# Fused attention, gated convolution and mixing MLP on one core: new ranks, new delays, and a head's first score moved by one place

## The chip, the cores and the metric

One NeuronCore of a Trainium2 chip. The metric is device microseconds of one execution of the whole program; a kernel's time is the median of its runs. Engines are named as in the profile: PE (TensorE matmuls), PEld (its weight loads), DVE (VectorE), ACT (ScalarE), POOL (GpSimd), SP (the queue that issues DMAs).

## What is computed

Three blocks follow each other, with B = 4 batches, 8 heads, sequence 576, head size 64, model size 512. Cut to what matters:

```python
scores = where(causal, -1e9, q @ k.T / 8 + minimum(-(cum_i - cum_j), 0))   # cum = cumsum(max(s, 0))
x = softmax(scores) @ v                      # 4 x 576 x 512, heads side by side
gate = sigmoid(causal_conv5(x, conv_w))      # 5 taps per channel
x = (gate * (x @ w_val)) @ w_out
u = x + (x.transpose(0, 2, 1) @ U @ V).transpose(0, 2, 1)    # rank 32 mixing over the sequence
out = u + maximum(u @ w_ch1, 0) @ w_ch2      # 512 -> 2048 -> 512
```

## The kernel before

Everything lives transposed in one tile `uT` (128 channels x 4 x 2304 tokens). Dense matmuls are made exact enough by splitting each operand into a rounded high part and the rest (`xh`/`xl`, `gvh`/`gvl`, `nh`/`nl`, `hh`/`hl`, weights `..h`/`..l`) and adding three products. Weights arrive as 64-bit words and are widened to two float parts by POOL and DVE in small steps (`widen`, lines 368 to 389); the DVE steps on integers there are called shifts in this document.

The 32 heads are taken one after the other, two of them a pair. For head n, `score` makes five row blocks S0 to S4 of scores, each followed by a row maximum on DVE (written into `P`, with `nm`) and an exp on ACT. One head later `trans` transposes the five blocks (T0 to T4) on PE into `pt`, and ACT or DVE copies them into `PTA` and `PTB`. After an odd head `attn_v` multiplies the pair by V in two parts A0 (reads `PTA`) and A1 (reads `PTB`), into the single accumulator `av`. Then DVE scales it into `X` by the row sums (`rs`, `wrs`), five taps of the convolution are accumulated in `av` again (`tap`, line 609), and a tanh on ACT writes the gate from `av` into `uT` (line 621). So the next pair's A0 can't start before this tanh. In timeline rows the tanh is `uT<-av`, a tap is `av<-X,cw,av`.

When a batch's eight heads are through, its dense work is laid between the next batch's heads: `values` (x times w_val, `d<-xh,wvh`; gating makes `gvh` on ACT and `gvl` on DVE), `outputs` (`d<-gvh,woh`), and the mixing, in which `uT` is transposed, split into `nh` (ACT) and `nl` (DVE), multiplied by U, split into `ast` by ACT and then DVE, and multiplied by V (`d<-V4h,ast`). For batch 0 the dense products start at head 10, for batch 1 at head 18, for batch 2 at head 26; the mixing falls into heads 14 to 16, 22 to 24 and 30 to 31. The last batch's dense work stands alone, with some MLP units laid between (`beside`, line 943), and from about 376 us only the MLP is left.

The order of the work is set three times over. The program emits steps on a clock of its own: ORDER and ORDER0 (lines 89, 90, used at line 785) give the order of scores, transpositions and products of a head, ORDER where the head being transposed is odd; `defer` (line 156) puts a step off by a delay from DT; SIDE, DENSE, R0 to R3 say how much side work goes between. Then a scheduler orders each engine's queue, and a kind's rank decides there: every operation goes through `Via` (line 118), which takes engine and rank from PLAN, or from FIRST for heads 0 to 8, and issues it with that priority (line 132). Last, each engine runs its queue in order. PSUM is short: six buffers `d` are shared by scores, transpositions and dense groups.

Lines: all operations with a rank other than 0 have line 132 (`Via`); with rank 0 they have the line of the call: 139 to 143 (`rnd`), 148 (`rest`), 375 (a POOL step of `widen`), 614 (a tap). In the changed kernel every line is 35 higher.

Of the kernel before, what the change touches and what calls it, by code (L numbers as in the profile page):

```python
# [19 lines left out]
DRAM = bass.MemoryType.DRAM  # L20


PLAN = {
    "pace": ("gpsimd", 0),
    "qk_hi": ("gpsimd", 2000),
    "qk_lo": ("gpsimd", 2000),
    "put": ("sync", 3000),
    "wd_rest": ("gpsimd", 100),
    "xh": ("gpsimd", 0),
    "xl": ("gpsimd", 500),  # L30
    "gh": ("scalar", 6000),
    "gl": ("vector", 0),
    "uh": ("gpsimd", -2000),
    "ul": ("gpsimd", -6000),
    "u4": ("vector", 0),
    "wd_a": ("gpsimd", 0),
    "wd_lim": ("gpsimd", 0),
    "wd": ("vector", -2000),
    "wd_hi": ("gpsimd", -2000),
    "wd_lo": ("gpsimd", 2000),  # L40
    "s": ("tensor", -6000),
    "max": ("vector", -2000),
    "exp": ("scalar", 6000),
    "t": ("tensor", 500),
    "pt00": ("scalar", 0),
    "pt10": ("scalar", 6000),
    "pt20": ("scalar", -500),
    "pt30": ("scalar", -6000),
    "pt40": ("scalar", -6000),
    "pt41": ("vector", 6000),  # L50
    "av": ("tensor", 6000),
    "rs": ("vector", -500),
    "wrs": ("gpsimd", 2000),
    "t_rb": ("tensor", 500),
    "rb": ("scalar", 6000),
    "x": ("vector", 2000),
    "tap0": ("scalar", 100),
    "tap": ("vector", 0),
    "tanh": ("scalar", -100),
    "d": ("tensor", 2000),  # L60
    "gv": ("vector", -100),
    "ox": ("scalar", 0),
    "tm": ("tensor", 6000),
    "nh": ("scalar", 0),
    "nl": ("vector", 100),
    "ah": ("scalar", -100),
    "al": ("vector", 0),
    "um": ("vector", 0),
    "c1": ("tensor", 100),
    "c2": ("tensor", -2000),  # L70
    "hh": ("scalar", 0),
    "hl": ("vector", 6000),
    "acc": ("vector", 6000),
}
R0 = 0.0
R1 = 0.0
R2 = 0.4
R3 = 6.0
DENSE = 36.0
DWAIT = 3.0  # L80
GROUPS = [2, 2, 3, 4, 3, 2]
RING = 7
PACED = False
SIDE = [7, 7, 3, 7]
WHOLE = [0, 1, 2, 3, 4, 5, 6, 7, 16, 30]
PB = [1, 1, 1, 2, 2]
XB = 1
FIRST = {"pt41": ["scalar", 500], "nl": ["vector", 500], "xh": ["gpsimd", 2000], "c2": ["tensor", 100], "max": ["vector", 2000], "rs": ["vector", 500], "t": ["tensor", 100], "rb": ["vector", 500], "av": ["tensor", 6000], "wd_rest": ["gpsimd", 2000]}
ORDER0 = "T0 S0 T1 T4 S1 T3 T2 S2 S3 S4"
ORDER = "T0 T1 S0 T2 T3 S1 S2 S3 T4 S4 A0 A1"  # L90
NPD = 6
DT = {"exp": 0.51, "xh": 0.96, "xl": 0.25, "tap": 1.5, "taps": 0.9, "tanh": 1.83, "gv": 4.3, "nl": 3.6, "rows": 10.0, "prep": 1.51}
WARM = 13


# [1 line left out]
def fused_kernel(ctx, tc, qT, kT, vP, s, wval, wout, convw, U, V, w1, w2, rows01, out):  # L97
# [20 lines left out]
    class Via:  # L118


        def __init__(self, kind):
            self.name, self.ahead = FIRST.get(kind, PLAN[kind]) if PLAN[kind][0] != "sync" and phase[0] <= 8 else PLAN[kind]
            self.engine = getattr(nc, self.name)
# [11 lines left out]
    def rnd(kind, o, i, by=1.0):  # L135

        eng = Via(kind)
        if eng.name == "scalar":
            eng.mul(o, i, by)  # L139
        elif eng.name == "vector" and by == 1.0:  # L140
            eng.tensor_copy(o, i)
        else:
            eng.tensor_scalar(o, i, by, 0.0, op0=ALU.mult, op1=ALU.add)
# [12 lines left out]
    def defer(dt, f, key=None):  # L156
        order[0] += 1
        later.append((clock["now"] + dt, order[0], f, key))
# [17 lines left out]
    def side_step(n=1):  # L176
        while n and side_work:
            more = side_work.popleft()()
            if isinstance(more, list):
                side_work.extendleft(reversed(more))  # L180
            else:
                n -= 1
# [7 lines left out]
    def advance(cost):  # L190
        clock["now"] += cost
        while later:
            x = min(later, key=lambda y: y[:2])
            if x[0] > clock["now"]:
                break
            later.remove(x)
            x[2]()
# [286 lines left out]
    def score(n, c):  # L484
# [26 lines left out]
        def exp():  # L511
# [4 lines left out]
            ready.add(("P", n, c))  # L516
        defer(DT["exp"] + W / 960.0, exp, "sc")

# [71 lines left out]
    def norm(pr):  # L590
# [8 lines left out]
        def split_hi():  # L599
            xh[b, p] = db.tile([P, S], F32R, tag=f"xh{p}", name=f"xh{p}", bufs=2 if p < XB else 1)  # L600
            xl[b, p] = db.tile([P, S], F32R, tag=f"xl{p}", name=f"xl{p}", bufs=2 if p < XB else 1)
            rnd("xh", xh[b, p], X[:, 4:])
            defer(DT["xl"], split_lo)

# [4 lines left out]
        def tap(k):  # L609

            if k == 0:
                Via("tap0").mul(g, X[:, 0:S], cw[:, p, 0:1])
            else:
                Via("tap").scalar_tensor_tensor(  # L614
                    g, X[:, k:k + S], cw[:, p, k:k + 1], g, op0=ALU.mult, op1=ALU.add,
                )
            defer(DT["taps"], lambda: tap(k + 1) if k < 4 else gate())

        def gate():

            Via("tanh").activation(G(b, p), g, AF.Tanh, scale=0.5)
            ready.add(("G", b, p))
        defer(DT["xh"], split_hi)
        defer(DT["tap"], lambda: tap(0))

# [19 lines left out]
    def values(b):  # L645
        halves = [slice(0, HS), slice(HS, S)]
        need(*[("wide", c) for c in range(NP)])
        until(*[("x", b, p) for p in range(NP)])
        for hf, cols in enumerate(halves):
            for m in range(NP):  # L650
                ps = psD.tile([P, 512], F32, tag="d", name="d")
                yield from products(
                    ps[:, 0:HS], wv, m, [xh[b, p][:, cols] for p in range(NP)], [xl[b, p][:, cols] for p in range(NP)],
                )
                until(("G", b, m))
                tmp = ps[:, 0:HS]
                Via("gv").scalar_tensor_tensor(tmp, G(b, m)[:, cols], 1.0, tmp, op0=ALU.add, op1=ALU.mult)
                gh = gvh[m, hf] = da.tile([P, HS], F32R, tag=f"gvh{m}{hf}", name="gvh")
                gl = gvl[m, hf] = da.tile([P, HS], F32R, tag=f"gvl{m}{hf}", name="gvl")

                def split(tmp=tmp, gh=gh, gl=gl, key=("gv", b, m, hf)):
                    rnd("gh", gh, tmp)
                    rest("gl", gl, tmp, gh)
                    ready.add(key)
                defer(DT["gv"], split)
        yield 0.0
# [95 lines left out]
    for n in range(NH + 1):  # L762
# [21 lines left out]
        ahead, before = n < NH, n > 0  # L784
        for x in (ORDER if m % 2 else ORDER0).split():
            kind, i = x[0], int(x[1])
# [20 lines left out]
        for cost, f, a in items:  # L807
# [3 lines left out]
            if n > 0:  # L811
                steps[0] += SIDE[(n > 8) + (n > 12) + (n > 17)] * cost / total
                side_step(int(steps[0]))
# [129 lines left out]
    def beside(gen, share):  # L943

        nonlocal owed
        for cost in gen:
            advance(cost)
            owed += R3 if cost == LULL else share
            while owed >= 1.0:
                next(first_blocks, None)  # L950
                owed -= 1.0

    while len(dense) > 1:
        beside(dense.pop(0)[1], 0.0)
    beside([0.0], R0)
    beside(values(B - 1), R1)
    advance(20.0)
    ctx_b.close()
    wb = ctx.enter_context(tc.tile_pool(name="wb", side="right", **reuse))
    beside(outputs(B - 1), R2)  # L960
    for k in (4, 5):
# [55 lines left out]
```

## Time and profile before

| | us |
|---|---|
| median of 3 runs | 757.72 |
| lowest, highest of the 3 | 756.76, 767.9 |
| the profiled execution | 759.31 |
| its span | 757.5 |
| TensorE busy in it | 732.2 |

The profiled execution is the one whose rows are read below. Its time includes 1.8 us around the span of the instructions. Times in rows are microseconds from the start of the span; in timeline rows the second number is the duration of the row's instructions and the square brackets tell how long the engine was idle before the row and what released it.

### The profile page before, as it was taken

To read this page: it belongs to the slowest core of one execution; us is meant where nothing else is said; L and a number is where in the kernel's file an instruction comes from. 1 tells how busy PE (TensorE), PEld (TensorE's weight loads), DVE (VectorE), ACT (ScalarE), POOL (GpSimd) and SP (SyncE) were. 2 spreads that over 40 slices of the span, in tenths; PEclk is the share of its full clock that TensorE was granted. 3 is DMA by queue.
4 is the path that set the end of the run, shared out by engine and by line. 5 is a ranking of instruction groups with operands and counts; after the bars stand their busy time and mean duration, and the time that the engine had idled before them with its cause. 6 is when DMAs were issued, how large, how long until landed. Compare 5 with 4: busy or idle time off the path is not lost.

```text
span 757.5 us, 12149 instructions
## 1 busy us (share of the span) xinstructions
PE 732.2 (97%) x4369; PEld 617.7 (82%) x4369; DVE 449.5 (59%) x1053; ACT 264.7 (35%) x718; POOL 340.8 (45%) x393
## 2 busy tenths in 40 slices
PE   8988999899999999999999999999999999999998
PEld 5666879678988998798788888888888888888887
DVE  6888887887668656651546776764462233323234
ACT  6776566756677567422110110110011011001110
POOL 2777677566544143550086877862660024100000
PEclk9999999999999999899999999999999999999999
DMA  4675354644556441010002222220120000000033
GB/s 121 188 200 160 90 136 111 174 118 128 143 130 154 107 98 35 29 57 1 0 1 84 84 84 82 86 83 29 34 79 28 1 29 0 1 1 1 0 112 139
DMA packets 27000, 59.39 MB, mean 78 GB/s; under 512 B 4648, under 2 KB 5288, under 8 KB 26940
## 3 DMA queue, kind: packets, MB, share of 16 engines
q1 hardware_dynamic: 26940, 58.61, 27.8%
q8 instruction: 35, 0.57, 0.3%
q14 instruction: 25, 0.20, 0.1%
HBM read 37.04 MB, written 5.31 MB: 56 GB/s over the span
## 4 chain that ended last, share of the span: by engine, by line
PE 85%; DVE 5%; DMA 3%; ACT 2%; POOL 2%; issue 1%; SPq 1%; POOLq 0%; DVEq 0%; ACTq 0%
PE d L132 42%; PE acc L132 26%; PE pt L132 7%; PE sc L132 5%; PE av L132 5%; DVE uT L132 2%; DVE P L132 1%; DMA qk<-in_kT 1%; DMA uT<-in_w 1%; DVE av L614 1%; DMA K<-Q 1%; ACT P L132 1%; SPq L132 0%; ACT PTA L132 0%; DMA K<-uT 0%
## 5 line engine op out<-in xcount | busy, mean ns | idle before, releaser
L132 PE MATMUL d<-u,w1h 128*128 128x512 f32 (+1 forms) x640 | 184.2, 371 | 0.0
L877 ACT ACTIVATE hh<-d 128x512 fp32r<-128x512 f32 (+1 forms) x80 | 44.1, 556 | 343.0 <-PE acc L132 177.3
L132 DVE SCALAR_TENSOR_TENSOR hl<-d,hh 128x512 fp32r<-128x512 f32 (+1 forms) x80 | 50.7, 635 | 152.9 <-ACT hh L877 152.8
L132 PEld LDWEIGHTS d<-u,w1h 128*128 128x128 f32 x640 | 116.1, 188 | 22.4
L132 PE MATMUL d<-u,w1l 128*128 128x512 f32 (+1 forms) x320 | 118.7, 371 | 0.0
L132 PE MATMUL acc<-hl,w2h 128*128 128x512 f32 (+1 forms) x320 | 104.5, 370 | 0.0
L132 PE MATMUL acc<-hh,w2h 128*128 128x512 f32 (+1 forms) x320 | 104.3, 371 | 0.2 <-DVE uT L132 0.2
L132 ACT ACTIVATE P<-P,nm 128x576 f32<-128x576 f32 (+4 forms) x160 | 89.1, 560 | 36.1 <-DVE nm L132 35.2
L132 PE MATMUL acc<-hh,w2l 128*128 128x512 f32 (+1 forms) x320 | 101.1, 369 | 0.0
L132 DVE TENSOR_TENSOR uT<-acc,uT 128x512 f32<-128x512 f32 (+1 forms) x120 | 70.1, 630 | 35.7 <-PE acc L132 30.4
L132 PE MATMUL sc<-K,Q 68*128 68x288 f32 (+13 forms) x384 | 87.3, 342 | 1.9 <-ACT PTA L139 1.8
L132 PE MATMUL pt<-ident,P 128*128 128x128 f32 x480 | 76.4, 284 | 5.2 <-ACT P L132 3.0
L132 DVE CUSTOM_DVE_ANT_0 P<-sc,causal 64x64 f32<-64x64 f32 (+4 forms) x160 | 64.9, 420 | 23.6 <-PE sc L132 21.4
L132 PEld LDWEIGHTS sc<-K,Q 68*128 68x128 f32 (+2 forms) x384 | 62.0, 193 | 9.3 <-ACT PTA L139 2.2
L132 PEld LDWEIGHTS d<-u,w1l 128*128 128x128 f32 x320 | 60.3, 188 | 11.2
L132 PEld LDWEIGHTS acc<-hh,w2h 128*128 128x128 f32 x320 | 58.8, 188 | 11.5 <-issue 0.6
L132 PEld LDWEIGHTS acc<-hl,w2h 128*128 128x128 f32 x320 | 59.0, 188 | 11.0 <-DVE hl L132 0.3
L132 PEld LDWEIGHTS acc<-hh,w2l 128*128 128x128 f32 x320 | 58.7, 188 | 10.5
L132 PEld LDWEIGHTS pt<-ident,P 128*128 128x128 f32 x480 | 54.8, 143 | 13.7 <-ACT P L132 5.4
L614 DVE SCALAR_TENSOR_TENSOR av<-X,cw,av 128x576 f32<-128x576 f32 x64 | 52.2, 815 | 3.0 <-ACT av L132 2.7
L132 DVE TENSOR_SCALAR scr<-scr 128x512 uint32<-128x512 uint32 x56 | 29.0, 519 | 29.9 <-POOL w1l L132 20.2
L132 ACT ACTIVATE PTB<-pt 128x384 f32<-128x384 f32 (+1 forms) x72 | 37.0, 522 | 10.3 <-PE pt L132 10.0
(125 smaller groups left out, 1285.5 us busy)
## 6 DMA issues: line engine op xcount, KB each, us to landing
raw<-in_w SPq DMA_DIRECT2D x28, 512.0 KB
K<-hi SPq DMA_DIRECT2D x44, 144.0 KB
Q<-hi SPq DMA_DIRECT2D x44, 144.0 KB
V<-in_vP SPq DMA_DIRECT2D x16, 320.0 KB
out<-uT SPq DMA_DIRECT2D x16, 256.0 KB
qk<-in_qT SPq DMA_DIRECT2D x22, 144.0 KB
qk<-in_kT SPq DMA_DIRECT2D x22, 144.0 KB
K<-Q SPq DMA_DIRECT2D x22, 144.0 KB
```

The source lines that it names most:

```text
L132: return f(*args, **kw)
L614: Via("tap").scalar_tensor_tensor(g, X[:, k:k + S], cw[:, p, k:k + 1], g, op0=ALU.mult, op1=ALU.add,)
L877: Via("hh").activation(h_, o, AF.Relu)
```

## The change

Only constants at the top of the file change; functions stay. The ranks in PLAN get other numbers (the engines stay), FIRST grows from 10 to 29 kinds, and these change:

```diff
-R0 = 0.0
+R0 = 0.13
-R2 = 0.4
-R3 = 6.0
+R2 = 0.38
+R3 = 9.68
-SIDE = [7, 7, 3, 7]
+SIDE = [7, 7, 2, 6]
-    "wd": ("vector", -2000),
+ 'wd': ['vector', 0],
-    "exp": ("scalar", 6000),
+ 'exp': ['scalar', -2000],
-ORDER = "T0 T1 S0 T2 T3 S1 S2 S3 T4 S4 A0 A1"
+ORDER = 'T0 S0 T1 T2 T3 S1 S2 S3 T4 S4 A0 A1'
-DT = {"exp": 0.51, "xh": 0.96, "xl": 0.25, "tap": 1.5, "taps": 0.9, "tanh": 1.83, "gv": 4.3, "nl": 3.6, "rows": 10.0, "prep": 1.51}
+DT = {'exp': 0.76,
+ 'xh': 0.72,
+ 'xl': 0.57,
+ 'tap': 1.65,
+ 'taps': 0.7,
+ 'tanh': 3.22,
+ 'gv': 4.08,
+ 'nl': 0.66,
+ 'rows': 8.9,
+ 'prep': 2.52}
```

So in ORDER the next head's S0 stands before T1 where it stood after it.

What that moves is told by the order of the engines' queues. On DVE, in the second head of the first mixing stage (head 15), this stood before; the TENSOR_SCALAR and SCALAR_TENSOR_TENSOR on `uT` are shifts of a weight slice, `P_92` is a score block with its maximum, `X_94` the scaled pair:

```order
L132 ISA P_92,nm<-sc,causal,nm 128x288
L132 ISA nm 128x1
L132 TENSOR_SCALAR uT<-uT 128x256
L132 SCALAR_TENSOR_TENSOR uT<-uT 128x256
L132 TENSOR_TENSOR nl<-pt,nh 128x512
L132 TENSOR_SCALAR uT<-uT 128x256
L132 SCALAR_TENSOR_TENSOR uT<-uT 128x256
L132 TENSOR_TENSOR X_94<-av,wrs 128x576
```

and this stands there now:

```order
L167 ISA P_92,nm<-sc,causal,nm 128x288
L167 ISA nm 128x1
L167 TENSOR_TENSOR nl<-pt,nh 128x512
L411 TENSOR_SCALAR uT<-uT 128x256
L167 TENSOR_TENSOR X_94<-av,wrs 128x576
L412 SCALAR_TENSOR_TENSOR uT<-uT 128x256
```

`nl` and `X` passed the shifts.

On ACT, in the same mixing stage (head 16), before; `P_91` and `P_87` are exps, `uT<-av` is the tanh:

```order
L132 ACTIVATE P_91,sums_97<-P_91,nm 128x448
L132 ACTIVATE PTA<-pt 128x3x128
L132 ACTIVATE ast<-d 128x512
L132 ACTIVATE PTB<-pt 128x4x128
L132 ACTIVATE uT<-av 128x576
L132 ACTIVATE P_87,sums_96<-P_87,nm 64x64
```

and now:

```order
L167 ACTIVATE PTA<-pt 128x3x128
L167 ACTIVATE ast<-d 128x512
L167 ACTIVATE uT<-av 128x576
L167 ACTIVATE P_87,sums_96<-P_87,nm 64x64
L167 ACTIVATE PTB<-pt 128x4x128
```

The tanh stands right behind `ast`, ahead of the `PTB` copy.

On ACT, where the dense products of batch 1 start (head 18), before:

```order
L132 ACTIVATE P_93,sums_96<-P_93,nm 128x576
L132 ACTIVATE uT<-av 128x576
L132 ACTIVATE gvh<-d 128x288 x2
L139 ACTIVATE PTA<-pt 128x64
L132 ACTIVATE PTA<-pt 128x2x128
L132 ACTIVATE gvh<-d 128x288 x2
L132 ACTIVATE PTA<-pt 128x3x128
L132 ACTIVATE P_87,sums_97<-P_87,nm 64x64
```

and now:

```order
L167 ACTIVATE P_93,sums_96<-P_93,nm 128x576
L174 ACTIVATE PTA<-pt 128x64
L167 ACTIVATE uT<-av 128x576
L167 ACTIVATE gvh<-d 128x288 x3
L167 ACTIVATE PTA<-pt 128x2x128
L167 ACTIVATE P_87,sums_97<-P_87,nm 64x64
L167 ACTIVATE PTA<-pt 128x3x128
```

The small `PTA` copy moved ahead of the tanh; three `gvh` and the exp now stand ahead of the last `PTA` copy, where four `gvh` and no exp stood.

## Rows read from the trace of the kernel before

**Rows 1.** The page: busy time of each engine over the span.
```profile
PE 732.2 (97%) x4369; PEld 617.7 (82%) x4369; DVE 449.5 (59%) x1053; ACT 264.7 (35%) x718; POOL 340.8 (45%) x393
```

**Rows 2.** Chain of waits, a dense stretch: start, us, engine and tile.
```profile
480.23 8.39 PE d L132 x36
```

**Rows 3.** Windows of the last stop before the values and of the MLP.
```profile
core 0: us, PE busy (x) PEld busy (x) DVE busy (x) ACT busy (x) POOL busy (x), PEclk, DMA share, GB/s
304.00:319.00 15.00, 13.52 (x80) 10.25 (x79) 9.64 (x25) 6.68 (x17) 7.60 (x7) 0.77 0.01 2
376.00:757.00 381.00, 378.23 (x1832) 316.34 (x1831) 184.99 (x305) 41.14 (x75) 149.38 (x152) 1.00 0.14 48
```

**Rows 4.** Waits of PE, 80 to 400 us: us in total, times, longest.
```profile
PE d L132 <- DVE ast L148: 2.4, 2, 1.5
PE av L132 <- ACT uT L132: 2.3, 2, 1.2
...
PE acc L132 <- DVE uT L132: 0.2, 1, 0.2
```

**Rows 5.** Timeline, 135 to 140 us, head 15.
```profile
135.22 0.60 ACT L139 ACTIVATE nh<-pt 128x512 fp32r<-128x512 f32 x1 [0.71 <-PE pt L132]
...
135.62 0.43 POOL L143 TENSOR_SCALAR uT<-uT 128x256 f32<-128x256 f32 x1 [3.01 <-DMA uT<-in_w]
...
136.49 1.40 POOL L132 TENSOR_TENSOR Q<-qk,hi 128x576 fp32r<-128x576 f32 x1
136.56 1.48 DVE L132 TENSOR_SCALAR uT<-uT 128x256 uint32<-128x256 uint32 x1 [1.31 <-POOL uT L375]
...
138.88 0.68 DVE L132 TENSOR_TENSOR nl<-pt,nh 128x512 fp32r<-128x512 f32 x1
...
139.49 0.28 DVE L132 TENSOR_SCALAR uT<-uT 128x256 uint32<-128x256 uint32 x1
139.62 0.51 PE L132 MATMUL d<-nl,U 128*128 128x512 f32 x1 [0.77 <-DVE nl L132]
```

**Rows 6.** Timeline, 146 to 150 us, head 16.
```profile
146.88 0.85 DVE L132 TENSOR_SCALAR uT<-uT 128x256 uint32<-128x256 uint32 x1
...
147.65 0.81 DVE L614 SCALAR_TENSOR_TENSOR av<-X,cw,av 128x576 f32<-128x576 f32 x1
147.72 0.59 ACT L132 ACTIVATE ast<-d 128x512 fp32r<-128x512 f32 x1
...
148.20 0.60 ACT L132 ACTIVATE PTB<-pt 128x512 f32<-128x512 f32 x1
...
148.68 0.67 ACT L132 ACTIVATE uT<-av 128x576 f32<-128x576 f32 x1
...
149.40 1.20 PE L132 MATMUL av<-PTA,V 128*64 128x320 f32 x12 [1.07 <-ACT uT L132]
```

**Rows 7.** Timeline, 156 to 160 us, head 17.
```profile
156.17 0.29 DVE L132 TENSOR_SCALAR uT<-uT 128x256 uint32<-128x256 uint32 x1 [0.72 <-POOL uT L375]
...
159.85 0.74 PE L132 MATMUL pt<-ident,P 128*128 128x128 f32 x5 [0.52 <-DVE nm L132]
```

**Rows 8.** Timeline, 108.6 us, the first score of head 12.
```profile
108.64 0.41 PE L132 MATMUL sc<-K,Q 68*128 68x64 f32 x2 [0.40 <-ACT PTA L139]
```

**Rows 9.** Timeline, 169 to 173 us, head 18.
```profile
169.39 0.65 ACT L132 ACTIVATE uT<-av 128x576 f32<-128x576 f32 x1 [1.27 <-DVE av L614]
...
170.24 0.77 ACT L132 ACTIVATE gvh<-d 128x288 fp32r<-128x288 f32 x2 [0.20 <-DVE d L132]
...
170.90 0.22 ACT L139 ACTIVATE PTA<-pt 128x64 f32<-128x64 f32 x1
...
171.17 0.41 PE L132 MATMUL sc<-K,Q 68*128 68x64 f32 x2 [1.36 <-ACT PTA L139]
...
172.48 0.34 ACT L132 ACTIVATE P<-P,nm 64x64 f32<-64x64 f32 x1
...
172.88 0.49 PE L132 MATMUL av<-PTA,V 128*64 128x320 f32 x2
```

More of the change, by code (lines that the diff above doesn't have):

```diff
@@ L20 @@
 DRAM = bass.MemoryType.DRAM
[L23 to L37, printed above, removed]
-    "wd": ("vector", -2000),
[L39 to L42, printed above, removed]
-    "exp": ("scalar", 6000),
[L44 to L74, printed above, removed]
@@ L75 @@
-R0 = 0.0
+PLAN = {'pace': ['gpsimd', -100],
+ 'qk_hi': ['gpsimd', 2000],
+ 'qk_lo': ['gpsimd', 100],
+ 'put': ['sync', 3000],
+ 'wd_rest': ['gpsimd', 0],
+ 'xh': ['gpsimd', 100],
+ 'xl': ['gpsimd', -2000],
+ 'gh': ['scalar', -2000],
+ 'gl': ['vector', 0],
+ 'uh': ['gpsimd', 2000],
+ 'ul': ['gpsimd', -500],
+ 'u4': ['vector', 0],
+ 'wd_a': ['gpsimd', 6000],
+ 'wd_lim': ['gpsimd', 0],
+ 'wd': ['vector', 0],
+ 'wd_hi': ['gpsimd', -6000],
+ 'wd_lo': ['gpsimd', 2000],
+ 's': ['tensor', -6000],
+ 'max': ['vector', -100],
+ 'exp': ['scalar', -2000],
+ 't': ['tensor', 500],
+ 'pt00': ['scalar', 0],
+ 'pt10': ['scalar', 6000],
+ 'pt20': ['scalar', 100],
+ 'pt30': ['scalar', 2000],
+ 'pt40': ['scalar', 2000],
+ 'pt41': ['vector', 6000],
+ 'av': ['tensor', 6000],
+ 'rs': ['vector', 2000],
+ 'wrs': ['gpsimd', -500],
+ 't_rb': ['tensor', 2000],
+ 'rb': ['scalar', -2000],
+ 'x': ['vector', -500],
+ 'tap0': ['scalar', 500],
+ 'tap': ['vector', 100],
+ 'tanh': ['scalar', -100],
+ 'd': ['tensor', -6000],
+ 'gv': ['vector', 2000],
+ 'ox': ['scalar', -2000],
+ 'tm': ['tensor', 500],
+ 'nh': ['scalar', 0],
+ 'nl': ['vector', 100],
+ 'ah': ['scalar', -6000],
+ 'al': ['vector', 500],
+ 'um': ['vector', 0],
+ 'c1': ['tensor', 100],
+ 'c2': ['tensor', -500],
+ 'hh': ['scalar', 0],
+ 'hl': ['vector', 6000],
+ 'acc': ['vector', -500]}
@@ L87 @@
 XB = 1
-FIRST = {"pt41": ["scalar", 500], "nl": ["vector", 500], "xh": ["gpsimd", 2000], "c2": ["tensor", 100], "max": ["vector", 2000], "rs": ["vector", 500], "t": ["tensor", 100], "rb": ["vector", 500], "av": ["tensor", 6000], "wd_rest": ["gpsimd", 2000]}
-ORDER0 = "T0 S0 T1 T4 S1 T3 T2 S2 S3 S4"
-ORDER = "T0 T1 S0 T2 T3 S1 S2 S3 T4 S4 A0 A1"
-NPD = 6
-DT = {"exp": 0.51, "xh": 0.96, "xl": 0.25, "tap": 1.5, "taps": 0.9, "tanh": 1.83, "gv": 4.3, "nl": 3.6, "rows": 10.0, "prep": 1.51}
+FIRST = {'pt41': ['scalar', 500],
+ 'nl': ['vector', 500],
+ 'xh': ['gpsimd', 0],
+ 'c2': ['tensor', -6000],
+ 'max': ['vector', 2000],
+ 'rs': ['vector', 500],
+ 't': ['tensor', 100],
+ 'rb': ['vector', 500],
+ 'av': ['tensor', 6000],
+ 'wd_rest': ['gpsimd', 2000],
+ 'ah': ['scalar', 0],
+ 'pt10': ['scalar', 0],
+ 'al': ['vector', 500],
+ 'xl': ['gpsimd', 500],
+ 'pt40': ['scalar', -2000],
+ 'gv': ['vector', 6000],
+ 'd': ['tensor', -2000],
+ 'pt00': ['scalar', 0],
+ 'gl': ['vector', 6000],
+ 'gh': ['scalar', 100],
+ 'hl': ['vector', 6000],
+ 'wd_hi': ['gpsimd', -6000],
+ 'u4': ['vector', -500],
+ 'pt20': ['scalar', -6000],
+ 'pace': ['gpsimd', -6000],
+ 'tm': ['tensor', -6000],
+ 'tap': ['vector', -2000],
+ 'qk_lo': ['gpsimd', -100],
+ 'wrs': ['gpsimd', 100]}
+ORDER0 = 'T0 S0 T1 T4 S1 T3 T2 S2 S3 S4'
+ORDER = 'T0 S0 T1 T2 T3 S1 S2 S3 T4 S4 A0 A1'
+NPD = 6
+DT = {'exp': 0.76,
[8 more added lines that the diff above has]
+ 'prep': 2.52}
 WARM = 13
```

## Prediction

> **What bounds the kernel now.** I read the page first. TensorE is busy for 732.2 of 757.5 us [rows 1], so only time in which it stands still, or runs at the lower clock, can be won or lost by a change of order. Busy time alone doesn't tell where, since records of neighbouring matmuls overlap. In the dense part 36 matmuls of 512 columns take 8.39 us, 0.233 us each [rows 2]. So I looked for the stretches in which that rhythm breaks. From 376 us to the end it does not: TensorE is busy for 378.23 of 381 us at the full clock [rows 3]. What can move lies before that.
>
> The waits of TensorE between 80 and 400 us come next: eleven lines, from 2.4 us for the mixing operand `ast` down to 0.2 us, 11.9 us together [rows 4]. A second loss is the clock. From 304 to 319 us the granted clock is 0.77 [rows 3]: 23% of 15 us, times two, is 6.9 us at the lower level of 1.2 GHz, which costs 3.4 us of work. TensorE had been stopping for `ast` and for copies just before. So all that another order could win after 80 us is about 11.9 + 3.4 = 15.3 us, 2% of the time. Before 80 us (heads 0 to 7) the order barely changes on any engine, and I count nothing there.
>
> **The change part by part.** Each engine issues the same instructions, of the same kinds and sizes, and the same number of DMAs. Only places change. SP's queue keeps its order but for neighbours that swap, so no transfer starts in another phase. I therefore price four places where TensorE waits in the profile, at the waits' own lengths.
>
> *DVE, the first mixing stage (head 15).* DVE is an in-order queue. At 135.62 POOL starts the first step on a weight slice, 3.01 us late because the slice's DMA was late. DVE's shift of that slice stands idle for 1.31 us and then takes 1.48 us; only after it and one more step comes `nl` at 138.88, for which TensorE waits 0.77 us at 139.62 [rows 5]. The change puts `nl` ahead of the shift. `nh` was there at 135.22 + 0.60 = 135.82, so `nl` can end two microseconds earlier: the whole 0.77 us goes. What is late next is the `wrs` transposes, which don't depend on `nl`. Term: -0.77, bounds 0 and -0.8.
>
> *ACT, the same stage, head 16.* TensorE waits 1.07 us at 149.40 for the tanh (`uT<-av`), because the accumulator that the next pair's product needs is the tanh's input. On ACT the tanh (148.68) stood behind a `PTB` copy of 0.60 us that began at 148.20; `ast` (147.72) is ahead of both. Its input, the last tap at 147.65 on DVE, stood behind a shift of 0.85 us at 146.88 [rows 6]. The change puts the tanh right behind `ast` and the shift behind the tap. The tanh can then start when the `PTB` copy did: 148.68 - 148.20 = 0.48 us earlier. The mixing matmuls behind it need DVE's `ast` step, which also moves up. The displaced `PTB` copy is needed only by the second half of the pair's product. Term: -0.48, bounds 0 and -1.07. In the next two mixing stages the tanh passes one copy and another passes it, so I count nothing.
>
> *DVE, head 17.* A shift waits 0.72 us for POOL at 156.17, with the row maximum of the last score behind it; later TensorE stands 0.52 us at 159.85 for a maximum [rows 7]. The change puts the maximum ahead, so its half microsecond falls into the idle time. Term: -0.4, bounds 0 and -0.52.
>
> *The first score.* In the odd-head order the next head's first score now precedes the second transposition (the diff moves it one place forward). At 108.64 that score waited 0.40 us for a copy [rows 8]. Two 64-column matmuls now cover part of what the transposition waits for: I take -0.2, bounds 0 and -0.4.
>
> *ACT, the start of a batch's dense products (heads 10, 18, 26).* Here the change can cost. In head 18 the order was: tanh 169.39, two `gvh` roundings 170.24, the small `PTA` copy 170.90; the score waited for that copy until 171.17 (1.36 us), and the next pair's first product ran at 172.88 [rows 9]. Now the small copy is ahead of the tanh, so that wait goes; but three `gvh` stand ahead of the next `PTA` copy, and an exp ahead of the last, which the first product needs. Two `gvh` took 0.77 us, so a third adds 0.4, and the exp 0.34; against this the last copy loses the fourth `gvh` that stood before it. I find the product ready at 172.8 to 173.9, and it was at 172.88: the gap moves from the score to the product. Term 0, bounds -1.4 and +1.0 a place.
>
> The other edits (the early MLP units laid among the last batch's output products, the ranks of the MLP's weight steps) fall in stretches where TensorE already runs without named waits. They cost nothing as long as the weights stay ahead; the order of POOL's weight steps there is the same but for two neighbours, and without that lead a unit would wait for one such step, about the 1.40 us of POOL's two-input step in [rows 5].
>
> Sum: -0.77 - 0.48 - 0.4 - 0.2 = -1.85 us. The profiled execution took 759.31 us (span 757.5), 1.6 us above the median of 757.72; it would become 757.5, and the median 755.9. I say 755.8.
>
> A row speaks against taking all of it: the 256-wide shift took 1.48 us while POOL ran a two-input step of 1.40 us, and 0.28 us alone three microseconds later [rows 5]. So a DVE step that the change puts beside another POOL step can grow by 1.2 us. The Trainium skill, SBUF: State Buffer, section "SBUF: two separate sides", says that GpSimd and VectorE take one port pair as an exclusive lock for a whole instruction, the loser standing still. The two ends agree with that here (138.04 and 137.89). Its sum would be the first rival's.
>
> **The rivals.** *The gains are eaten.* The moved shifts and the taps behind them meet POOL's two-input steps: two new meetings cost 2.4 us against 1.85 won, 758.3. For it: POOL is at work for most of the stretch, and orders were changed on both engines. Against: the moved steps are the less urgent ones.
>
> *Slower.* At the three dense starts the copies behind `gvh` and the exp hold up the first product by 1.0 us each, and one such stop costs the clock as at 309: 3.0 + 3.4 = 6.4 us, with none of the gains 764.1. It decides from the point where the delay exceeds what TensorE has queued before the product; in head 18 nothing dense stands there. Against: in head 26 twelve products do, of 288 columns each: 12 x 0.233 x 288/512 = 1.6 us by [rows 2], more than the delay.
>
> *Faster.* The stop before 309 is broken up (`ast` is one copy earlier on ACT) and the clock stays up: 1.85 + 3.4, 752.5. Against: DVE's step on `ast` keeps its place there, and it was what TensorE waited for.
>
> That the change does less than its long table says is a part of all of these: before 80 us and after 376 it moves next to nothing.
>
> **How the numbers follow.** Forecast 0.35; gains eaten 0.25; slower 0.20; faster 0.15; the rest, 0.05, for something that I don't see. Range: from the faster case less the bounds of head 16 and one dense start (752.5 - 0.6 - 1.4, and 2 us for the spread of the runs shown) 748.5, taken as 748; to the slower case, 764. The forecast's own range is 753 to 759. Two per cent, about what a measurement of this kernel can tell from no change, is 15.2 us: faster than 742.6 would need all the waits and the clock, slower than 772.9 more than twice the slow rival. So 0.04, 0.90 and 0.06.
>
> **What would show it.** Right: `nl` in head 15 no longer behind the shift, and no wait of TensorE for it; the wait for the tanh in head 16 shorter by about half; in head 18 no wait for the small copy but one for the larger `PTA` copy before the product; the clock still down once near 309; the stretch from 376 unchanged. Wrong: TensorE waits after 80 us well above 11.9 us or under 8; a further fall of the clock; a wait for weights in the MLP; or a change of over 2 us before 80 us.

## The result and the profile after

| | before | changed |
|---|---|---|
| median of 4 runs, us | 757.55 | 747.19 |
| lowest, highest | 756.76, 767.9 | 747.03, 747.49 |
| profiled execution, us | 759.31 | 747.34 |
| its span | 757.5 | 745.6 |

The 767.9 stands alone: the highest of 111 further executions of this kernel is 764.0. The ratio is 0.9853, with a 95% interval from 0.9818 to 0.9888: 10.4 us off the median. The forecast was 755.8 with a range from 748.0 to 764.0, so the direction was right, the size was not, and the time fell just below the range.

The page of the changed kernel has this row, which answers to [rows 1]:

```profile
PE 725.7 (97%) x4369; PEld 615.0 (82%) x4369; DVE 446.6 (60%) x1053; ACT 266.8 (36%) x718; POOL 340.0 (46%) x393
```

TensorE is busy for 6.5 us less with the same instructions. Less time at the lower clock is a part of that; the rest, which would be records of matmuls that overlap more, was not taken apart. The windows of the changed kernel, both 12 us earlier than in [rows 3] (columns: length, busy us of each engine with instructions, granted clock, DMA share, GB/s), show the clock's part. They end at the same work as those of before; the first begins some 3.5 us of work earlier, so it holds more matmuls:

```profile
292.00:307.00 15.00, 13.60 (x107) 11.29 (x106) 12.43 (x32) 9.84 (x26) 10.12 (x10) 1.00 0.09 23
364.00:745.00 381.00, 377.87 (x1830) 315.99 (x1828) 184.43 (x305) 41.14 (x75) 147.70 (x152) 1.00 0.14 48
```

The fall of the clock at the last stop before the values (0.77 in [rows 3]) is gone. The MLP, 381 us long in both, is as it was. TensorE's waits between 80 and 400 us, the view of [rows 4] (total us, times, longest), are now:

```profile
PE d L167 <- DVE ast L167: 2.7, 2, 1.4
PE av L167 <- ACT uT L167: 1.1, 2, 0.7
PE d L167 <- DVE gvl L183: 1.1, 1, 1.1
PE pt L167 <- DVE uT L748: 0.7, 1, 0.7
PE d L167 <- DVE nl L167: 0.4, 1, 0.4
...
PE av L167 <- ACT PTA L167: 0.2, 1, 0.2
PE sc L167 <- ACT PTA L174: 0.2, 1, 0.2
```

Its nine rows come to 7.0 us where the eleven of before came to 11.9. The waits for the tanh went from 2.3 to 1.1 us; the waits for `PTA` copies, 4.4 us before (1.8 for scores, 1.1 for transpositions, 1.5 for the product), shrank to 0.4. Two rows of before hold most of them:

```profile
PE sc L132 <- ACT PTA L139: 1.8, 2, 1.4
PE av L132 <- ACT PTA L132: 1.5, 1, 1.5
```

The profiled executions differ by 11.9 us of span: 4.9 by these waits and an estimated 3.4 by the clock at 309 us. The remaining 3.6 were not traced to single places. Some of it lies before 80 us, where the clock of the profiled execution of before also fell (0.83 between 70 and 80 us, 1.00 in the changed kernel), which costs up to 1.7 us. The changed kernel has a fall of its own at the very start (0.72 between 10 and 16 us); even so the pair's product that starts at 67.75 us before starts at 67.77 in it, and the one at 86.78 at 84.48. The rest lies in pauses too short for that view.

The timeline of the changed kernel, head 15 (start, duration, engine, operation, idle before and its releaser), answers to [rows 5]:

```profile
132.83 0.69 DVE L167 TENSOR_TENSOR nl<-pt,nh 128x512 fp32r<-128x512 f32 x1 [0.67 <-ACT nh L174]
...
134.91 0.40 POOL L410 TENSOR_SCALAR uT<-uT 128x256 f32<-128x256 f32 x1
...
135.34 0.30 DVE L411 TENSOR_SCALAR uT<-uT 128x256 uint32<-128x256 uint32 x1 [1.82 <-POOL uT L410]
...
135.55 0.75 DVE L167 TENSOR_TENSOR X<-av,wrs 128x576 f32<-128x576 f32 x1
```

The shift still waits for POOL, now for 1.82 us, but `nl` went through two and a half microseconds ahead of it. What stands behind the shift is `X`, for which TensorE doesn't stop here. In head 16, which answers to [rows 6]:

```profile
144.52 0.60 ACT L167 ACTIVATE ast<-d 128x512 fp32r<-128x512 f32 x1
...
145.01 0.64 ACT L167 ACTIVATE uT<-av 128x576 f32<-128x576 f32 x1
...
145.71 1.20 PE L167 MATMUL av<-PTA,V 128*64 128x320 f32 x12 [0.46 <-ACT uT L167]
...
145.87 0.58 ACT L167 ACTIVATE PTB<-pt 128x512 f32<-128x512 f32 x1
```

The tanh starts right behind `ast` and TensorE waits 0.46 us for it instead of 1.07. And in head 18, which answers to [rows 9]:

```profile
164.57 1.26 ACT L167 ACTIVATE gvh<-d 128x288 fp32r<-128x288 f32 x3
...
165.31 0.30 PE L167 MATMUL d<-xh,wvl 128*128 128x288 f32 x1
...
165.44 1.50 PE L167 MATMUL pt<-ident,P 128*128 128x128 f32 x9
...
166.56 0.49 ACT L167 ACTIVATE PTA<-pt 128x384 f32<-128x384 f32 x1
...
167.39 1.20 PE L167 MATMUL av<-PTA,V 128*64 128x320 f32 x12
```

Three `gvh` in a row do hold ACT for 1.26 us, as feared. But dense products stand on TensorE ahead of the transpositions, the last at 165.31; the 1.36 us stop of [rows 9] is gone, and no stop before the product has come in its place.

### The profile page after: what moved, and what is told of

Read it like the earlier page. It is cut to its first block, busy times and chain, and to the rows that moved or that the text cites. A ratio compares the mean times of both kernels' runs of the same rounds, so it can differ in the third digit from the quotient of the medians.

```text
span 745.6 us, 12129 instructions
## 1 busy us (share of the span) xinstructions
PE 725.7 (97%) x4369; PEld 615.0 (82%) x4369; DVE 446.6 (60%) x1053; ACT 266.8 (36%) x718; POOL 340.0 (46%) x393
## 4 chain that ended last, share of the span: by engine, by line
PE 86%; DVE 8%; ACT 2%; DMA 2%; issue 1%; POOL 1%; SPq 0%; DVEq 0%; POOLq 0%
PE d L167 40%; PE acc L167 27%; PE pt L167 8%; PE sc L167 6%; PE av L167 5%; DVE av L167 1%; DVE P L167 1%; DVE uT L416 1%; DMA uT<-in_w 1%; DVE uT L412 1%; ACT P L167 0%; DVE uT L411 0%; DMA Q<-in_qT 0%; DMA K<-hi 0%; ACT PTA L167 0%
## 5 line engine op out<-in xcount | busy, mean ns | idle before, releaser
L167 PE MATMUL acc<-hl,w2h 128*128 128x512 f32 (+1 forms) x320 | 107.4, 369 | 0.0
L167 PE MATMUL acc<-hh,w2h 128*128 128x512 f32 (+1 forms) x320 | 105.9, 370 | 0.2 <-DVE uT L167 0.2
L167 PE MATMUL acc<-hh,w2l 128*128 128x512 f32 (+1 forms) x320 | 105.0, 369 | 0.0
L167 PE MATMUL pt<-ident,P 128*128 128x128 f32 x480 | 74.3, 279 | 4.2 <-ACT P L167 2.7
L167 PEld LDWEIGHTS acc<-hl,w2h 128*128 128x128 f32 x320 | 58.9, 188 | 10.4
L167 PE MATMUL d<-gvh,woh 128*128 128x288 f32 x128 | 38.6, 309 | 1.1 <-DVE gvl L183 1.1
```

The costliest lines, as they stand in the source:

```text
L167: return f(*args, **kw)
```

## The experiments

Each run's times stand beside the kernel before on the same chip; "ratio" is against it, with its 95% interval. Diffs are against the kernel before, unless they say against the changed one.

**The kernel before again** (no edit).

> The kernel before, profiled a second time. Clock theory (the granted clock falls after TensorE has stopped several times in a few microseconds): the fall at 309 us, behind the stops at 306.4, 308.0 and 309.6, is there again, and the profile of 757 to 759 us holds it. Chance theory (the clock falls at times of its own): it stands elsewhere or is gone, and the time is about 3.4 us lower. For the shorter fall at 73.8 us I have no view; if it is gone, the span is about 1.7 us below 757.5.

Measured: 758.14 us (754.04 to 761.85, 10 runs); ratio 0.9981 (0.9956 to 1.0007). The clock fell near 309 again, though by half as much:

```profile
304.00:319.00 15.00, 13.51 (x92) 10.34 (x90) 10.58 (x28) 7.97 (x22) 8.72 (x8) 0.89 0.01 2
```

So that fall is not pure chance, and its length is not fixed. Nor does it come each time: the profiles of ORDER alone, the delays alone and the program alone, below, have none there. More telling is the spread: one program takes from 754 to 762 us, and this profile has a stop that the first one lacked, near 190 us. The timeline of this second profile:

```profile
190.52 1.42 POOL L132 TENSOR_TENSOR Q<-qk,hi 128x576 fp32r<-128x576 f32 x1
...
190.59 1.49 DVE L132 TENSOR_SCALAR uT<-uT 128x256 uint32<-128x256 uint32 x1 [0.66 <-POOL uT L375]
...
192.00 0.61 DVE L132 CUSTOM_DVE_ANT_0 P<-sc,causal 128x448 f32<-128x448 f32 x1
...
192.55 0.08 DVE L132 DVE_READ_ACCUMULATOR2_ANT nm<- 128x1 f32 x1
...
192.68 0.48 PE L132 MATMUL sc<-K,Q 68*128 68x64 f32 x2 [0.87 <-DVE nm L132]
```

and the same instructions in the first profile of before:

```profile
190.25 0.29 DVE L132 TENSOR_SCALAR uT<-uT 128x256 uint32<-128x256 uint32 x1
...
190.38 1.45 POOL L132 TENSOR_TENSOR Q<-qk,hi 128x576 fp32r<-128x576 f32 x1 [0.18 <-PE sc L132]
...
190.45 0.62 DVE L132 CUSTOM_DVE_ANT_0 P<-sc,causal 128x448 f32<-128x448 f32 x1
...
190.99 0.09 DVE L132 DVE_READ_ACCUMULATOR2_ANT nm<- 128x1 f32 x1
```

The reader is to see one program and two outcomes. Where the shift starts 0.13 us before POOL's two-input step it takes 0.29 us; where it starts 0.07 us behind it, it waits the step out and takes 1.49. The last step of the row maximum behind it starts 1.96 us after the shift's start instead of 0.74, and TensorE stops for 0.87 us. [rows 5] held the same pair of durations; here the maxima stand behind it.

**Only the ranks; only what the program emits; only ORDER; only the delays.** The first takes PLAN and FIRST from the changed kernel, the second all the rest (R0, R2, R3, SIDE, ORDER, DT). The third and fourth are one line each:

```diff
-ORDER = "T0 T1 S0 T2 T3 S1 S2 S3 T4 S4 A0 A1"
+ORDER = "T0 S0 T1 T2 T3 S1 S2 S3 T4 S4 A0 A1"
```

```diff
-DT = {"exp": 0.51, ..., "rows": 10.0, "prep": 1.51}
+DT = {"exp": 0.76, ..., "rows": 8.9, "prep": 2.52}
```

> Only the ranks (PLAN and FIRST); delays, ORDER, R0, R2, R3 and SIDE as before. Rank theory (each engine issues the urgent step first, as the prediction argued): most of the gain is here, 749 to 752 us, with the waits for nl, tanh and PTA shorter. Laying theory (TensorE has other work when a step is late, since the program lays the steps elsewhere): under 3 us of gain, 755 to 759 us.

> Only what the program emits in another order (delays DT, ORDER, R0, R2, R3, SIDE); ranks as before. Rank theory: under 3 us of gain, 755 to 759 us. Laying theory: most of the gain, 748 to 752 us.

> Only ORDER, so the next head's first score one place earlier; all else as before. By the prediction's term -0.2 us: 757.3, within 0.5 us of before. If the first score is what fills the stop in front of the transpositions in each odd head (some 12 heads after 80 us, 0.3 us each), 753 to 755.

> The kernel before with the new delays alone; of the ten only rows moves any instruction. Additive theory (rows is worth 6 us wherever it stands): 751 to 753. Joint theory (rows helps only where the first score is early too): 756 to 758.5.

| | us | ratio, interval |
|---|---|---|
| only ranks | 759.15 | 1.0015 (0.9986 to 1.0044) |
| only program | 755.70 | 0.9975 (0.9949 to 1.0002) |
| only ORDER | 757.67 | 0.9993 (0.997 to 1.0015) |
| only delays | 755.29 | 0.998 (0.9957 to 1.0003) |

Neither half has the gain, and the halves don't add up to it: +1.3 and -2.2 us against -10.4. None of the four intervals excludes that nothing changed. Both theories of the first pair fall as they were put, and the delays alone, at 2.4 us, lie between both of theirs. ORDER alone gave 0.2 us, the very term of the prediction; but the interval reaches from 2.3 us won to 1.1 lost, so that it agrees is luck. The ranks alone show how a half can lose; their timeline at 155 us:

```profile
154.31 0.42 POOL L132 TENSOR_SCALAR uT<-uT 128x256 f32<-128x256 f32 x1 [2.02 <-DMA uT<-in_w]
154.81 0.40 POOL L375 TENSOR_SCALAR uT<-uT 128x256 f32<-128x256 f32 x1
155.25 0.29 DVE L376 TENSOR_SCALAR uT<-uT 128x256 uint32<-128x256 uint32 x1 [2.54 <-POOL uT L375]
...
156.78 0.41 DVE L132 COPY PTB<-pt 128x256 f32<-128x256 f32 x1
...
157.25 1.83 PE L132 MATMUL av<-PTB,V 128*64 128x192 f32 x12 [2.54 <-DVE PTB L132]
```

A slice's DMA is late, POOL waits for it, DVE's shift waits for POOL, and behind the shift stands a `PTB` copy for which TensorE then stops for 2.54 us. Right behind that stop the granted clock drops (the window of that kernel):

```profile
157.00:162.00 5.00, 4.75 (x31) 3.69 (x31) 3.02 (x10) 1.05 (x3) 2.68 (x5) 0.66 0.52 143
```

**The changed kernel again, and with one part put back.** Against the changed kernel: ORDER put back; DT put back (of its ten delays only `rows` moves an instruction in the queues, and the table FIRST moves none); R0, R2, R3 and SIDE put back.

> The changed kernel, timed beside the next three and profiled a second time. The granted clock fell near 309 us in two profiles of before and in none of the changed kernel. If the stop there is too short now for a fall of the clock: 747 us again, no fall between 20 us and the last microseconds. If that was chance: a fall there, 749 to 751.

> The changed kernel with ORDER alone put back. Since ORDER alone on before gave nothing (757.67 beside 757.85), additive theory: 747 to 748. Joint theory (the new ranks need the first score early, since they put other steps ahead of the copies it waits for): 750 to 753.

> The changed kernel with the delays DT alone put back. Ranks alone and program alone gave +1.3 and -2.2 us where both gave -10.4, so some part of the program works only with the ranks. Theory delays (the ranks' order on ACT and DVE is right only when tanh and nl are emitted at the new times): 753 to 758. Theory side work (R and SIDE fill the stops): 747 to 750.

> The changed kernel with R0, R2, R3 and SIDE alone put back. Theory side work: 752 to 757, TensorE again without dense work at the stops of heads 16, 18 and 24. Theory delays: 747 to 749.

| | us | lowest, highest | ratio, interval |
|---|---|---|---|
| changed, again | 747.16 | 746.89, 748.25 | 0.9862 (0.9826 to 0.9897) |
| ORDER back | 753.43 | 749.43, 755.66 | 0.993 (0.9903 to 0.9956) |
| delays back | 753.97 | 750.77, 758.97 | 0.9959 (0.993 to 0.9988) |
| R and SIDE back | 747.92 | 747.43, 749.22 | 0.9872 (0.9829 to 0.9916) |

Side work matters little. ORDER and `rows` cost over 6 us each when they alone are put back, and the spread of 6 to 8 us returns with them. With ORDER put back the profile is of the fastest execution (749.43) and has no stop of over 1.4 us, so it doesn't show where the others lose. The timeline with the delays put back shows the same chain as above, with a row maximum behind the shift:

```profile
131.61 0.41 POOL L132 TENSOR_SCALAR uT<-uT 128x256 f32<-128x256 f32 x1 [2.07 <-DMA uT<-in_w]
...
132.53 0.29 DVE L376 TENSOR_SCALAR uT<-uT 128x256 uint32<-128x256 uint32 x1 [2.61 <-POOL uT L375]
...
132.74 0.35 DVE L132 CUSTOM_DVE_ANT_0 P<-sc,causal 128x192 f32<-128x192 f32 x1
...
133.16 0.44 PE L132 MATMUL pt<-ident,P 128*128 128x128 f32 x2 [2.02 <-DVE nm L132]
```

and the window around it shows the clock:

```profile
130.00:137.00 7.00, 4.98 (x28) 3.48 (x28) 4.10 (x15) 3.62 (x11) 2.92 (x6) 0.77 0.62 153
```

A stop of 2.02 us, and behind it the lower level for 23% of 7 us, times two, 3.2 us, which costs another 1.6.

**One rank put back, and few numbers alone.** Against the changed kernel, d or wd is put back; against the kernel before, five numbers or two are taken over.

```diff
-    "d": ("tensor", -6000),
+    "d": ("tensor", 2000),
```

```diff
-    "wd": ("vector", 0),
+    "wd": ("vector", -2000),
```

> The changed kernel with one rank put back: d (the dense products on TensorE) 2000 for -6000. On TensorE's queue it spreads the dense products among transpositions and scores again, where the changed kernel lays them in blocks in front of them. Laying theory (a block of dense products covers the copies, maxima and exps that the next transposition waits for): 751 to 755, and single executions spread by some us. Rank theory of the prediction (DVE and ACT decide): 747 to 748.5.

> The changed kernel with one rank put back: wd (the shifts on DVE) -2000 for 0. Theory of the blocked DVE queue (a shift that waits for POOL, or runs 1.5 us beside POOL's two-input step, holds up the row maxima behind it, and TensorE stops): 749 to 753, with waits of TensorE for nm. If the dense blocks cover such stops: 747 to 748.5.

> The kernel before with five of the changed numbers: ORDER, the delay rows 8.9, the ranks d -6000, tm 500, wd 0. Everything else as before, the first heads' table too. If these carry the change: 747 to 749 and a spread under 1.5 us. If the gain needs the long table: 751 to 756.

> The kernel before with two of the changed numbers: ORDER and the delay rows (8.9 for 10). Putting back either cost about 6 us in the changed kernel, while ORDER alone gave 0.2 on before. If the two are enough together: 749 to 752. If they need d, tm and wd too: 754 to 758.

| | us | lowest, highest | ratio, interval |
|---|---|---|---|
| changed, d back | 748.94 | 748.23, 749.1 | 0.987 (0.9829 to 0.991) |
| changed, wd back | 748.39 | 747.32, 749.27 | 0.9863 (0.9822 to 0.9905) |
| before, five numbers | 749.50 | 748.25, 752.85 | 0.9886 (0.9838 to 0.9933) |
| before, ORDER and rows | 755.82 | 752.62, 759.36 | 0.9977 (0.9953 to 1.0001) |

Five numbers of the long table give 8.5 of the gain; their times reach 752.85, so the narrow spread that was expected of them did not come. Two give 1.9: ORDER and `rows` need the ranks. With d back, TensorE's waits between 80 and 400 us have this row, against 0.4 in the changed kernel and 0.9 in its second profile:

```profile
PE pt L132 <- DVE nm L132: 2.2, 4, 0.9
```

The block of dense products covers row maxima, as the laying theory had it, but the whole run is 1.7 us slower and not 4 to 8. With wd back the theory of the blocked queue asked for 749 to 753, and 748.39 came. The run is no test of it: it shows the same waits as the changed kernel, and on DVE it moves 6 of 1053 steps, all of them after 450 us. Nothing follows from its 1.2 us.

**Idle matmuls in a stop.** Ten matmuls of 256 columns, whose result is overwritten, in front of the mixing product that waits for `ast`; first in three batches, then in batch 2 alone (the diff), then that in the changed kernel.

```diff
+                for _ in range(10 if m + hf == 0 and b == 2 else 0):
+                    Via("tm").matmul(ps[:, 0:256], warm[:, 0:P], warm[:, 0:256], start=True, stop=True)
                 Via("tm").matmul(ps[:, 0:HS], lhsT, V4["h"][:, cols], start=True, stop=False)
```

> The kernel before, with ten matmuls of 256 columns that write nothing of use, set on TensorE between the last transposition and the mixing product that waits for ast (batches 0 to 2); their result is overwritten. TensorE so works through the 1.1 us stop at 309.6. Clock theory (the granted clock falls behind stops that come close together): no fall near 309 us, mean granted clock of the runs above that of before, 1 to 3 us less: 755 to 757. Otherwise the fall stays and the time is 757.5 to 759.

> The kernel before, with ten idle matmuls of 256 columns in front of one mixing product only, that of batch 2, at the stop of 309 us; up to there every queue stands as before. They cost about 1.1 us of TensorE and take the place of a stop of 1.1 us. Clock theory (the fall at 309 comes from the stops in front of it): no fall there, 1 to 3 us less than before, mean granted clock higher. If the fall is not tied to the stop: within 0.7 us of before.

> The changed kernel with the same ten idle matmuls in front of the mixing product of batch 2, where it stops for 1.5 us. Its profiles show no fall of the clock there. If a stop without a fall costs only itself: 747 to 747.5, the same. If executions without a profile have falls there: 0.5 to 1.5 less.

Measured: 754.08 in three batches (ratio 0.9951, 0.9917 to 0.9984), 757.94 in batch 2 alone (1.0, 0.9982 to 1.0017), 747.96 in the changed kernel (0.987, 0.9845 to 0.9894). The first is no clean test: from head 16 on, the scheduler laid other steps differently, on DVE too, so its 4 us can't be put down to the clock. The second is clean up to the stop. Its window has no fall,

```profile
300.00:316.00 16.00, 15.48 (x121) 12.74 (x119) 12.89 (x34) 10.24 (x28) 9.69 (x9) 1.00 0.07 22
```

and yet the median is that of before. The mean granted clock of its twelve executions is 0.9972, that of before beside them 0.9960: 0.9 us of span and not 3.4. So the fall at 309, which the prediction priced at 3.4 us, is not worth that over many executions, unless the idle matmuls cost elsewhere what they gave back; the run doesn't tell. Idle matmuls won nothing in the changed kernel either.

**Without the shifts.** The four DVE steps of eight weight slices are left out, in each kernel; nearly all else keeps its order.

```diff
         steps = widen(pairs(hraw), hscr, hi=w12[m][nm + "h"][:, cols], lo=w12[m][nm + "l"][:, cols])
+        steps[2:6] = [lambda: None] * 4
+        steps[8] = lambda: Via("wd_lo").tensor_add(w12[m][nm + "l"][:, cols], hscr[0], hscr[0])
```

> The kernel before without the four DVE steps of the eight weight slices of 256 that are widened between heads 13 and 21 (the shifts; left out: these slices' second float part, so the first two MLP units get other weights). 32 of 1055 DVE instructions, some 12 us of an engine that is busy for 450. Theory of the blocked queue (in the kernel before, shifts that wait for POOL stand ahead of maxima, nl and taps, and TensorE stops): 752 to 755, with less spread. If DVE's blocks cost nothing: 757 to 758.5.

> The same steps left out of the changed kernel. Theory of the blocked queue (there the shifts wait as long, but nothing urgent stands behind them): 746 to 747.2, so the gain is under a third of that on the kernel before. If shifts cost both kernels alike, the gain is the same in both.

Measured: 751.46 us (750.42 to 754.0), ratio 0.9922 (0.9895 to 0.995), from the kernel before; 748.39 us (745.84 to 751.48), ratio 0.9877 (0.9847 to 0.9907), from the changed one. Taken out of the kernel before, 32 short steps of an engine that is busy for 59% of the span give 6.1 us and halve the spread; 751.46 is just under the expected 752 to 755. Taken out of the changed kernel they give nothing (748.39 beside 747.16 and 747.19, where 746 to 747.2 was expected); its spread even grew, and its profile has a new stop of 1.8 us for a rounding on POOL. A part of that is the clock: the mean granted clock of its six executions is 0.9955, against 0.9988 of the changed kernel, and its profile has 10 us at the lower level from 51 to 61 us (0.50), long before the first step that was left out. Of executions with a mean clock of 0.998 or more, the median goes from 756.9 to 750.8 us in the kernel before (50 and 5 executions) and from 747.1 to 746.3 in the changed one (7 and 2): 6.1 us against 0.8. This is the pair that settles most. TensorE's waits of the kernel before without shifts, 80 to 400 us, begin with

```profile
PE d L132 <- DVE ast L148: 2.4, 2, 1.5
PE av L132 <- ACT uT L132: 2.3, 2, 1.2
PE av L132 <- ACT PTA L132: 1.7, 1, 1.7
```

and none for `nl` or `nm` is left. DVE's own waits between 80 and 345 us say why the changed kernel doesn't care. First before, then changed:

```profile
DVE uT L132 <- POOL uT L375: 5.5, 5, 2.2
```

```profile
DVE uT L411 <- POOL uT L410: 7.2, 5, 2.1
```

The shifts of the changed kernel wait for POOL longer than those of before. What differs is what is queued behind them. One rival the pair leaves: leaving the steps out also frees DVE of 15 us of work (449.5 us busy, then 434.6) and POOL of waits for them. The changed kernel is rid of the same and gains little, so the work by itself is not worth 6 us.

No kernel tried that does all the work is faster than the changed one.

## Why the prediction was wrong

*The ceiling held.* 15.3 us was named as all that another order could win after 80 us; 10.4 came. The range did not: its low end took the faster rival, with head 16 and one of the three dense starts at their bounds, and left the other bounds out. All the bounds together (2.8 for the four terms, 4.2 for the starts, 3.4 for the clock) would have reached 747.3; that this is the measured time is luck, since the time was not won by these amounts.

*Of the four priced terms two came in part.* The tanh in head 16 was taken at -0.48; its wait went from 1.07 to 0.46. (The one in head 24, counted at nothing, went from 1.2 to 0.7 as well.) `nl` was taken at -0.77: it passed the shift as read, but TensorE waits 0.4 us for it, at another place. In place of the wait for a maximum in head 17 (-0.4) stands one of 0.7 us for a mixing add, so that term gave nothing. ORDER, at -0.2, can't be judged: alone it gave 0.2 with the interval above, and taken out of the changed kernel it costs 6. Of the signs of being wrong, one came: the waits after 80 us, 7.0 us, are under 8.

*The step that failed first is "I therefore price four places".* It took one profiled execution for the kernel. The block of DVE's queue by a shift that waits for POOL, or runs beside its two-input step, was in [rows 5] and [rows 7], and was priced where it happened to stop TensorE in that execution: 0.77 and 0.4 us. The runs show that one program meets it at other places in other executions (near 190 us in the second profile), and that without the shifts the kernel before is 6.1 us faster. The term is not two waits but the whole class. At 6.1 us for the class against 1.17 for the two, it was short by about 5 us; that is an estimate, since a shift that is left out is not the same as one that others pass. The 1.48 us row was even read with the wrong sign: as a threat of new meetings, the first rival, where it was a cost of the kernel before that the change takes off the path.

*The second is "Term 0" at the dense starts.* The delay of the `PTA` copies by `gvh` came, 1.26 us for three, and stopped nothing. The waits of 1.36 (head 18) and 1.46 us (head 10) for `PTA` are gone but for 0.21: some 2.6 us more than the term, of which a longer wait for `gvl` takes 0.5 back in the first profile and nothing in the second. The slower rival fell with it. "In head 18 nothing dense stands there" was read from the order of before; the change also lays the dense products in a block ahead of the transpositions. That cover is a part of it: with d put back, a wait of 0.94 us for `PTA` returns in head 18. But it is not the whole. In head 10 ORDER alone does most of it (transpositions just ahead wait 0.41 and 0.19 us there; one waits 0.41 in the changed kernel). First before, then with ORDER alone:

```profile
86.78 1.20 PE L132 MATMUL av<-PTA,V 128*64 128x320 f32 x12 [1.46 <-ACT PTA L132]
```

```profile
86.84 1.20 PE L132 MATMUL av<-PTA,V 128*64 128x320 f32 x12 [0.30 <-ACT PTA L132]
```

And the stop of head 18 begins at a shift. In [rows 9] the tanh, with the copies queued behind it, waits 1.27 us for the last tap on DVE. Five us earlier, before:

```profile
164.47 1.44 POOL L132 TENSOR_TENSOR xl<-X,xh 128x576 fp32r<-128x576 f32 x1
164.54 1.51 DVE L132 TENSOR_SCALAR uT<-uT 128x256 uint32<-128x256 uint32 x1 [0.51 <-POOL uT L375]
...
165.97 0.81 DVE L614 SCALAR_TENSOR_TENSOR av<-X,cw,av 128x576 f32<-128x576 f32 x1
```

The taps stood behind that shift. In the kernel before without shifts the same score starts without a wait:

```profile
166.07 0.39 PE L132 MATMUL sc<-K,Q 68*128 68x64 f32 x2
```

So a part of what this term missed belongs to the first step. With d put back 1.7 us return in all; how much of that is the cover was not taken apart.

*The third is the clock.* "The clock still down once near 309" was wrong; the faster rival had that right, by a reason that did not hold, since DVE's step on `ast` is as late as it was. But 3.4 us was the price in one execution. Over 111 executions of before, the mean granted clock is 0.996, 3.0 us of span lost if all of it were work; over eight of the changed kernel it is 0.9988, 0.9 us. A fit over those of before gives 0.78 us of time for each such microsecond. So the clock is about 2.1 x 0.78 = 1.7 of the 10.4 us. That is a correlation, and the runs with idle matmuls neither confirmed nor excluded it. But the rest of the gain does without the clock: the fourteen executions of before with a mean clock of 1.000 have a median of 755.2 us, the three such of the changed kernel 747.2, 8.0 us apart. The falls above stand behind stops of 2.54 and 2.02 us, the one near 309, 306 or 312 behind three shorter ones, in four profiles (the two of before, the ranks alone, ORDER with `rows`). A stop does not bring a fall each time: twelve profiles have one of 2.1 us that ends between 41.3 and 41.8 us, and in seven of them the clock falls between 41.0 and 42.9.

*Additive working failed as well.* The sum of terms assumed that each edit is worth the same wherever it stands. Ranks alone lose 1.3 us (within their interval, and at a mean clock of 0.9926) and two numbers alone give 1.9, yet each of the two is worth over 6 when the rest is there. The traces give a reason: each half leaves a late slice somewhere with a copy or a maximum behind the shift, and one such place costs a stop of 2 us or more and often the clock. That this is the reason in every execution was not shown; only the places in the profiles were. For the same reason the parts named above overlap: the 6.1 us of the shifts hold a part of the clock's 1.7 and of the dense starts.

## What to carry to other kernels

Where an engine's queue holds steps that wait for a slow supplier, look at what stands behind them, at every such place, not only at the waits of the bottleneck in one trace: the same block moves from execution to execution. If one program's times spread by over 1%, profile it twice before an order is priced, and compare what the two show. And price a reordering by taking the blocking steps out, since single edits of an order don't add up.

## What the runs showed of the hardware

A DVE shift of 256 columns takes 0.29 us when it starts 0.13 us before a two-input step of POOL, and 1.49 us when it starts 0.07 us behind one, ending 0.14 us after it, in the same program. The row maximum of 448 columns takes 0.62 us beside that same kind of POOL step and 0.61 without it, so not every DVE step is held up. The Trainium skill, SBUF — State Buffer, section "SBUF: two separate sides", has the loser of a shared port pair stand still for a whole instruction, and counts a DVE step in only if it runs in a 2-port mode or reads two operands from SBUF. The maximum agrees with that, since it reads its scores from PSUM. The shift reads one operand, so it agrees if it runs in such a mode, which no run here shows. The pair of durations was in the trace of before; that two tenths of a microsecond decide between them from one execution to the next was not expected.

The time of one program spread from 754.0 to 764.0 us over the executions of before, and from 746.9 to 748.3 in the changed kernel (111 and 8 executions): a better order was also a steadier one.
